# Chunked scan and two gated layers on one core: decays spread in float32, fillers on TensorE, 512-column tiles and a new early order

## The chip, the cores and the metric

The kernel runs on one core of a Trainium2 chip. The metric is the device time of one execution in microseconds (us), measured outside the kernel; the profile gives the span from the first to the last instruction of one profiled execution, which is a little shorter.

## What is computed

Three stages, cut to what matters:

```python
# 1. chunked scan, for each batch (4) and head (8); S = 768, D = 32, N = 16
log_a = np.log(np.clip(a, 1e-06, 1.0))
# per chunk: cum = cumsum(log_a), L = exp(cum_i - cum_j) for i >= j
y = ((C @ B.T) * L) @ x + (C @ state) * exp(cum)
state = exp(cum_last) * state + sum_j B_j x_j exp(cum_last - cum_j)
# 2. gated layer, 3072 tokens, 256 -> 1536 -> 256
g = x @ w_gate; x = (g * sigmoid(g) * (x @ w_val)) @ w_out
# 3. squared-ReLU layer, 256 -> 2048 -> 256
h = np.maximum(x @ w_in, 0.0); out = (h * h) @ w_out2
```

The weights arrive as 64-bit floats and are turned into float32 on the chip.

## The kernel before

**Scan.** `chunks` cuts each batch of 768 tokens into six chunks of 112 and one of 96, 28 in all, worked in order by `chunk_ops`. For chunk k TensorE forms the scores `cb` (B times C), VectorE's scan (L578 for a half of four heads, L608 for all eight) forms the decays `L`, VectorE multiplies both into `mt` (L662, two halves), and TensorE's product `ys` (L676) of `mt` and `xa` gives the chunk's output and its next state, which goes through `st`, `turn` (L715) and back into `xa` (L718). There is one `mt` buffer. The first seven chunks (`EARLY`, batch 0) get the input of their scan in a special way: the clipped decays are cut into three bfloat16 parts that add up to the float32 value (`part_steps`, L251 to L261, on ScalarE and VectorE), and TensorE spreads them over 128 partitions with a 0/1 matrix `pick` (L569, eight matmuls a chunk); chunk 0 instead loads its decays with a broadcast DMA (L594) and clips them (L604). Later chunks load a broadcast copy from `decay` in DRAM.

**Gated layer.** `glu` works on one slice f of 128 hidden features (12 slices) and n tokens: products `g` and `v` (L729), tanh on ScalarE (L793), two VectorE operations (L796, L799), and the product `acc` (L847). In the "exact" form it uses plain float32 matmuls, 2 + 2 + 2 instructions of n columns (two passes each in the trace); otherwise both operands are cut into a high and a low part and it takes 6 + 6 + 6 matmuls of n columns, and GpSimd forms the low part of `t` (L820). Batch 0 is cut into cells (`PLAN["cells"]`: two slices, a range of chunks, exact or not). Batches 1 to 3 are done in tiles of 336 and 432 tokens.

**Weights.** A `Unit` is 1 MB of weights: two DMAs, two ScalarE operations (L406, L400), three on VectorE (L412, L417, L421); a split into high (L427, ScalarE) and low (L432, GpSimd) follows. Nine units feed the gated layer.

**Squared-ReLU layer.** `relu2`: per slice and 512 tokens six matmuls of 512 columns (`h`, L729) and twelve of 256 (`acc`, L920). At the end four `drain` operations copy the last accumulators into buffers of pool `tmp` (three buffers) and `store` sends them out (L955).

**Order.** `Graph.order` is a list planner: with a cost for each operation, priorities from `PLAN` and a count of buffers, it fixes in advance the order in which each engine's instructions stand. The engines then run their queues strictly in that order, with semaphores.

Of the kernel before, what the change touches and what calls it, by code (L numbers as in the profile page):

```python
# [34 lines left out]
class Graph:  # L35
# [14 lines left out]
    def order(self):  # L50
# [5 lines left out]
        avail, out, events, now = {}, [], [], 0.0  # L56
# [71 lines left out]
def kernel(  # L128
# [45 lines left out]
    pools = dict(w=20, raw=2, tmp=3, p=3, tr=3, L=2, ab=2, xf=1, bcr=1, st=2, ps=8)  # L174
# [7 lines left out]
    NBC, NX, NEB = 4, 3, 2  # L182
# [3 lines left out]
    pools["mt"] = 1  # L186
# [14 lines left out]
    decay = dram.tile([NB, NCB, H, Q + 1], F32, name="decay")  # L201

    def new(buf, shape, dtype, tag=None):
# [24 lines left out]

    def clip():
# [4 lines left out]
        nc.vector.tensor_scalar(  # L234
            dv[:, :full, 1:], ac[0 : 3 * R, : full * Q].rearrange("p (c q) -> p c q", c=full),
            1e-6, 1.0, op0=ALU.max, op1=ALU.min,
        )
        if full < NCB:
            nc.vector.tensor_scalar(
                dv[:, full, 1 : 1 + S - full * Q], ac[0 : 3 * R, full * Q : S],  # L240
                1e-6, 1.0, op0=ALU.max, op1=ALU.min,
            )

    e3 = ac[0 : 3 * R, : EARLY * (Q + 1)].rearrange("p (c q) -> p c q", c=EARLY)

    def part_steps(c0, c1):

        d, e, q = dv[:, c0:c1], e3[:, c0:c1], parts3[:, c0:c1]

        def one():  # L250
            nc.scalar.activation(q, d, AF.Copy)  # L251

        def two():
            nc.vector.tensor_tensor(e, d, q, op=ALU.subtract)

        def three():
            nc.scalar.activation(q[R : 2 * R], e[R : 2 * R], AF.Copy)
            nc.scalar.activation(q[2 * R :], e[2 * R :], AF.Copy)

        def four():  # L260
            nc.vector.tensor_tensor(q[2 * R :], e[2 * R :], q[2 * R :], op=ALU.subtract)  # L261

        return one, two, three, four

    def setup_pool():
        nc.gpsimd.memset(eye, 0.0)
# [24 lines left out]
    def setup_delta():  # L291
        nc.gpsimd.memset(delta, 0.0)
# [6 lines left out]
    def setup_pick():  # L299
        nc.gpsimd.memset(pick, 0.0)  # L300
        for i in range(3):
            nc.gpsimd.affine_select(
                out=pick, in_=pick, pattern=[[-1, H]], base=-i * R,
                channel_multiplier=1, compare_op=ALU.not_equal, fill=1.0,
            )
# [11 lines left out]
    def setup_mt():  # L317
        nc.gpsimd.memset(mt[:, :, Q:P], 0.0)

    xf_buf = Buf("xf")  # L320
    op_eye = g.add("POOL", 550, setup_pool, prio=-1000)
    op_eb = [g.add("POOL", 350, lambda i=i: setup_eb(i), prio=-999.5 + 0.1 * i) for i in range(NEB)]
    op_mask = g.add("POOL", 600, setup_mask, prio=-999)
    op_delta = g.add("POOL", 2000, setup_delta, prio=-998)
    op_mt = g.add("POOL", 200, setup_mt, prio=-997)
    op_pick = g.add("POOL", 900, setup_pick, prio=-996)
    op_bc = g.add("POOL", 1500, setup_bc, prio=-900)
    op_tab = g.add("ACT", 1500, act_table, prio=-990)
    op_pick.deps.append(op_tab)

    def dma(eng, n, cost, move, fn, deps=(), prio=0.0, bufs=()):

        i = g.add(eng, n * cost, fn, deps, prio, bufs, lat=0)
        return g.add("DMA", move, None, [i], prio, bufs, lat=1700)

    ld_a = dma("SP", 3, 450, 400, load_a, [], -950, setup_L)
    op_clip = g.add("DVE", 1250, clip, [ld_a], -950, setup_L)

# [5 lines left out]
    parts_done = {}  # L344
    first_parts = 3
    for c0, c1, prio in ((0, first_parts, -940), (first_parts, EARLY, 150)):
        f = part_steps(c0, c1)
        n = (c1 - c0) * (Q + 1)
        o1 = g.add("ACT", 220 + n * 0.83, f[0], [op_clip], prio, setup_L)
        o2 = g.add("DVE", 160 + n * 1.04, f[1], [o1], prio, setup_L)  # L350
        o3 = g.add("ACT", 2 * (220 + n * 0.83), f[2], [o2], prio, setup_L)
        o4 = g.add("DVE", 160 + n * 1.04, f[3], [o3], prio, setup_L)
        for c in range(c0, c1):
            parts_done[c] = o4
    kept = {
        b: dma("SP", 1, 450, 400, lambda b=b: keep_decays(b), [op_clip], 300 + b, setup_L)
# [84 lines left out]
    def chunk_ops(k, prio, after=(), load_after=()):  # L441
# [9 lines left out]
        c.mt = Buf("mt")  # L451
# [6 lines left out]
        load_after = [*load_after, before.load if before else None]  # L458
        free_x = ck[k - NX].y if k >= NX else None
        free_m = before.y if before else None  # L460
# [100 lines left out]
        if early and k:  # L561
            for i in range(HG):
                ps = Buf("ps")

                def spread(i=i, ps=ps):
                    v = new(ps, [P, G, Q + 1], F32, "ab")
                    for j in range(G):
                        h = i * G + j
                        nc.tensor.matmul(  # L569
                            v[:, j, :], pick[:, h : h + 1].to_broadcast([3 * R, P]), parts3[:, k, :],  # L570
# [12 lines left out]
                o = g.add("PE", 250, spread, [parts_done[k], op_pick, ck[k - 1].scans[-1]], prio, [ps, c.L], lat=250)  # L583
                s = g.add("DVE", 1080, scan, [o, op_delta, *scans], prio, [ps, c.L])
                scans = [s]
        else:
            ab = Buf("ab")

            def load_ab():
                v = new(ab, [P, H, Q + 1], F32, "ab")  # L590
                if early:
                    nc.vector.memset(v[:, :, 0:1], 0.0)
                    w = a[b, :, t : t + n]
                    nc.sync.dma_start(out=v[:, :, 1:], in_=bass.AP(w.tensor, w.offset, [[0, P], *w.ap]))  # L594
                else:
                    w = decay[b, t // Q].rearrange("h q -> (h q)")
                    nc.sync.dma_start(
                        out=v.rearrange("p h q -> p (h q)"),
                        in_=bass.AP(w.tensor, w.offset, [[0, P], *w.ap]),
                    )  # L600

            def hold():
                v = ab.t[:, :, 1:]
                nc.vector.tensor_scalar(v, v, 1e-6, 1.0, op0=ALU.max, op1=ALU.min)  # L604
# [494 lines left out]
```

## Time and profile before

| | us |
|---|---|
| device time, median of 3 runs | 674.58 (674.35 to 675.39) |
| the profiled execution, device time | 675.3 |
| its span | 673.6 |
| TensorE (PE) busy | 641.3, 95% |
| VectorE (DVE) busy | 418.6, 62% |
| ScalarE (ACT) busy | 337.7, 50% |
| GpSimd (POOL) busy | 224.1, 33% |

A busy share is an average over the span. The page's 40 slices show PE at 10, 60, 80 and 90% in its first four slices (17 us each), and at 90% or more from there to the last slice (60%). PEld is the loading of stationary operands and overlaps PE. Ends of matmuls are modelled, so that short gaps between matmuls count as busy; start times are recorded.

### The profile page before, as it was taken

What the parts mean: (1) busy time and instruction counts of PE and PEld (TensorE: products, weight loads), DVE (VectorE), ACT (ScalarE), POOL (GpSimd) and SP (SyncE); (2) the same over time, 40 slices, a digit from 0 to 9 for tenths busy, and PEclk for the clock granted to TensorE, in tenths of its full rate; (3) what the DMA queues carried; (4) which work ended last, traced back from release to release, by engine and by line L of the source; (5) the groups of instructions that cost most, each with busy time, mean ns of one, the idle gap of its engine ahead of it and who ended that gap; (6) DMA issues with size and microseconds to landing.
All of it is one profiled execution on the core that took longest, in us unless ns stands there. A gap on an engine that the chain in (4) does not pass through costs nothing.

```text
span 673.6 us, 11146 instructions
## 1 busy us (share of the span) xinstructions
PE 641.3 (95%) x4318; PEld 575.9 (85%) x4318; DVE 418.6 (62%) x598; ACT 337.7 (50%) x666; POOL 224.1 (33%) x226
## 2 busy tenths in 40 slices
PE   1689899999999999999999999999999999999996
PEld 1476498998998899988999989999999999999996
DVE  6899875456666665666468788554454544544543
ACT  6775554344545544545366665444444444444443
POOL 4353447546556564666255751100000000000000
PEclk9979999999999999999999999999999999999999
DMA  8868675206574747342521430000000000000000
GB/s 236 186 154 171 130 163 85 46 5 133 107 141 79 143 76 143 72 91 46 157 63 63 133 119 1 0 32 1 1 32 1 31 1 1 32 1 1 32 1 32
DMA packets 135749, 49.55 MB, mean 74 GB/s; under 512 B 121136, under 2 KB 124208, under 8 KB 135696
## 3 DMA queue, kind: packets, MB, share of 16 engines
q1 hardware_dynamic: 135408, 48.57, 32.6%
q8 instruction: 34, 0.56, 0.4%
q10 hardware_dynamic: 288, 0.26, 0.1%
q14 instruction: 19, 0.16, 0.1%
HBM read 34.59 MB, written 3.22 MB: 56 GB/s over the span
## 4 chain that ended last, share of the span: by engine, by line
PE 88%; DMA 4%; POOL 3%; ACT 2%; DVE 1%; SPq 1%; issue 1%; DVEq 0%; ACTq 0%; POOLq 0%
PE acc L920 20%; PE h L729 20%; PE g L729 15%; PE acc L847 14%; PE v L729 13%; PE ys L676 2%; POOL p L820 2%; DMA raw<-in_moe_w_val_dram 2%; PE cb L647 1%; DMA eb<-in_B_dram 1%; POOL lo L432 1%; PE cb L638 1%; DMA bct<-bcs 1%; PE turn L715 1%; ACT raw L406 1%
## 5 line engine op out<-in xcount | busy, mean ns | idle before, releaser
L920 PE MATMUL acc<-hi,p 128*128 128x256 f32 x768 | 152.5, 283 | 0.0
L820 POOL TENSOR_TENSOR p<-t,p 128x432 fp32r<-128x432 f32 (+2 forms) x88 | 102.5, 1168 | 103.7 <-ACT p L815 95.1
L920 PEld LDWEIGHTS acc<-hi,p 128*128 128x128 f32 x768 | 125.5, 191 | 4.0
L901 DVE TENSOR_TENSOR t<-t 128x512 f32<-128x512 f32 x96 | 69.8, 728 | 70.5 <-ACT t L898 70.4
L920 PE MATMUL acc<-lo,p 128*128 128x256 f32 x384 | 108.6, 283 | 0.0
L908 DVE TENSOR_TENSOR p<-t,p 128x512 fp32r<-128x512 f32 x96 | 66.2, 691 | 55.1 <-ACT p L904 54.9
L898 ACT ACTIVATE t<-h 128x512 f32<-128x512 f32 x96 | 57.2, 597 | 81.9 <-PE h L729 80.4
L796 DVE SCALAR_TENSOR_TENSOR t<-t,g 128x432 f32<-128x432 f32 (+3 forms) x102 | 53.4, 524 | 64.3 <-ACT t L793 63.6
L847 PE MATMUL acc<-p,hi 128*128 128x432 f32 (+2 forms) x352 | 92.2, 342 | 1.0 <-POOL p L820 0.9
L904 ACT ACTIVATE p<-t 128x512 fp32r<-128x512 f32 x96 | 60.5, 631 | 62.9 <-DVE t L901 61.7
L793 ACT ACTIVATE t<-g 128x432 f32<-128x432 f32 (+3 forms) x102 | 47.7, 469 | 58.2 <-PE g L729 56.3
L920 PEld LDWEIGHTS acc<-lo,p 128*128 128x128 f32 x384 | 73.4, 191 | 3.9
L729 PE MATMUL h<-xh_all,hi 128*128 128x512 f32 x192 | 76.5, 398 | 0.0
L729 PE MATMUL h<-xh_all,lo 128*128 128x512 f32 x192 | 76.2, 397 | 0.0
L729 PE MATMUL h<-xl_all,hi 128*128 128x512 f32 x192 | 76.2, 397 | 0.0
L815 ACT ACTIVATE p<-t 128x432 fp32r<-128x432 f32 (+2 forms) x88 | 45.6, 519 | 60.9 <-DVE t L799 59.2
L847 PEld LDWEIGHTS acc<-p,hi 128*128 128x128 f32 x352 | 61.9, 188 | 6.1 <-POOL p L820 2.4
L799 DVE SCALAR_TENSOR_TENSOR t<-t,v 128x432 f32<-128x432 f32 (+1 forms) x90 | 50.1, 557 | 26.0 <-PE v L729 19.6
L729 PE MATMUL g<-xh_all,hi 128*128 128x432 f32 (+2 forms) x184 | 64.3, 349 | 0.0
L729 PE MATMUL g<-xh_all,lo 128*128 128x432 f32 (+2 forms) x184 | 62.1, 337 | 0.4 <-POOL lo L432 0.4
L729 PE MATMUL g<-xl_all,hi 128*128 128x432 f32 (+2 forms) x184 | 61.8, 336 | 0.0
L432 POOL TENSOR_TENSOR lo<-v,hi 128x1024 fp32r<-128x1024 f32 x17 | 45.0, 2650 | 45.7 <-ACT hi L427 43.0
(97 smaller groups left out, 1165.1 us busy)
## 6 DMA issues: line engine op xcount, KB each, us to landing
ab<-decay SPq DMA_DIRECT2D x21, 452.0 KB, 4.7
raw<-in_moe_w_out_dram SPq DMA_DIRECT2D x14, 512.0 KB, 5.1
raw<-in_moe_w_in_dram SPq DMA_DIRECT2D x8, 512.0 KB, 4.4
raw<-in_moe_w_gate_dram SPq DMA_DIRECT2D x6, 512.0 KB, 4.1
raw<-in_moe_w_val_dram SPq DMA_DIRECT2D x6, 512.0 KB, 6.2
xa<-in_x_dram SPq DMA_DIRECT2D x24, 112.0 KB, 2.5
out_dram<-o SPq DMA_DIRECT2D x10, 256.0 KB, 2.2
bc<-in_B_dram SPq DMA_DIRECT2D x18, 56.0 KB, 4.3
```

The source lines that it names most:

```text
L432: e.tensor_tensor(self.lo.t, self.v.t, self.hi.t.bitcast(F32), op=ALU.subtract)
L729: nc.tensor.matmul(ps, l, r, start=(i == 0), stop=(i == len(terms) - 1))
L793: nc.scalar.activation(t[:, :n], gg(), AF.Tanh, scale=0.5)
L796: nc.vector.scalar_tensor_tensor(tb.t[:, :n], tb.t[:, :n], 1.0, gg(), op0=ALU.add, op1=ALU.mult)
L799: nc.vector.scalar_tensor_tensor(tb.t[:, :n], tb.t[:, :n], 0.5, vv(), op0=ALU.mult, op1=ALU.mult)
L820: e.tensor_tensor(p[:, 1, :n], tb.t[:, :n], p[:, 0, :n].bitcast(F32), op=ALU.subtract)
L847: nc.tensor.matmul(ps, l, r, start=bank not in done_f, stop=f == NF - 1, skip_group_check=True,)
L898: nc.scalar.activation(new(tb, [P, TN], F32, "t"), ph.t, AF.Relu)
L901: nc.vector.tensor_tensor(tb.t, tb.t, tb.t, op=ALU.mult)
L904: nc.scalar.activation(new(pb, [P, 2, TN], F32R, "p")[:, 0, :], tb.t, AF.Copy)
L908: e.tensor_tensor(pb.t[:, 1, :], tb.t, pb.t[:, 0, :].bitcast(F32), op=ALU.subtract)
L920: nc.tensor.matmul(ps, pb.t[:, l, tk], r, start=(f == 0 and s == 0 and q % 2 == 0), stop=(f == NF2 - 1 and s == 2), skip_group_check=True,)
```

## The change

- The decays are held once, in float32 and on all 128 partitions (`dv_all`; the rows above 32 are zeros), loaded straight into place by two DMAs and clipped there. The cutting into three parts, chunk 0's broadcast load and its clip are gone. All seven early chunks spread their decays on TensorE with a float32 `pick` matrix, 56 matmuls instead of 48 in bfloat16.
- Two `mt` buffers instead of one; four `tmp` buffers instead of three.
- Batches 1 to 3 in tiles of 256 and four times 512 tokens instead of six tiles of 336 and 432.
- Fillers: where the planner sees TensorE idle for 110 ns or more in its first 70 us, it puts matmuls of a bfloat16 tile of zeros (`idle`, 256 columns, one per 110 ns) ahead of the operation that waits, into the buffer that this operation then overwrites: 119 of them.
- Some clearing of tiles moves from GpSimd to VectorE ahead of the first data; planner costs and the starting clock change; one PSUM bank is no longer kept free; and `PLAN` is new, so that the early order of all engines differs.

The diff, cut to its core:

```diff
-    pools = dict(w=20, raw=2, tmp=3, p=3, tr=3, L=2, ab=2, xf=1, bcr=1, st=2, ps=8)
+    pools = dict(w=20, raw=2, tmp=4, p=3, tr=3, L=2, ab=2, xf=1, bcr=1, st=2, ps=8)
-    mt = const.tile([P, H, P], F32, name="mt")
+    mts = [const.tile([P, H, P], F32, name=f"mt{i}") for i in range(NMT)]
+    idle = const.tile([P, 256], BF16, name="idle")
-    pick = const.tile([3 * R, H], BF16, name="pick")
-    parts3 = const.tile([3 * R, EARLY, Q + 1], BF16, name="parts3")
+    pick = const.tile([P, H], F32, name="pick")
+    dv_all = const.tile([P, NCB, Q + 1], F32, name="dv")
+    dv = dv_all[0:R]
...
+        if buf.pool == "ps" and fills:
+            t = buf.t.rearrange("p a b -> p (a b)") if len(shape) == 3 else buf.t
+            t = t[:, : min(n, 256)]
+            for _ in range(fills.pop()):
+                nc.tensor.matmul(t, idle[:, : shape[0]], idle[:, : t.shape[-1]], start=True, stop=True)
...
-        free_m = before.y if before else None
+        free_m = ck[k - NMT].y if k >= NMT else None
...
-        if early and k:
+        if early:
...
-                            v[:, j, :], pick[:, h : h + 1].to_broadcast([3 * R, P]), parts3[:, k, :],
+                            v[:, j, :], pick[:, h : h + 1].to_broadcast([P, P]), dv_all[:, k, :],
...
-    tiles = [(b * S + o, b * S + e) for b in range(NB) for o, e in ((0, cut), (cut, S))]
+    over = (T - S) % TN
+    edges = [0, cut, S, *([S + over] if over else []), *range(S + over + TN, T + 1, TN)]
+    tiles = list(zip(edges, edges[1:]))
...
+            if op.eng == "PE":
+                if op.start < PLAN["warm"]:
+                    free = max([last] + [o.start + o.took + 250 for o in op.after if o is not None])
+                    if op.start - free >= 110:
+                        fills.append(int((op.start - free) / 110))
+                last = op.start + op.took
...
     cells=[
+        (5, 3, 7, 0),
+        (4, 0, 3, 0),
+        (5, 0, 3, 1),
...
+    spare=0,
+    warm=70000,
```

What it does to the queues, at the three places that matter below. First VectorE from the clip of the decays to the second chunk's `mt`. The rows before (L412, L417, L421 are one weight unit's three operations, L578 and L608 scans, `parts` the cutting into three):

```order
L254 TENSOR_TENSOR ac<-dc,parts_110 96x452
L261 TENSOR_TENSOR parts_110<-ac,parts_110 32x339
L412 SCALAR_TENSOR_TENSOR raw<-raw 128x1024
L417 TENSOR_SCALAR v<-v 128x1024
L421 SCALAR_TENSOR_TENSOR v<-v,raw 128x1024
L261 TENSOR_TENSOR parts_110<-ac,parts_110 32x452
...
L604 TENSOR_SCALAR ab<-ab 128x8x112
L608 SCALAR_TENSOR_TENSOR L<-ab,delta 128x904
L662 TENSOR_TENSOR mt<-cb,L 128x4x112 x2
L578 SCALAR_TENSOR_TENSOR L<-ab,delta 128x452 x2
```

And now, where L561 is the scan of a half, L634 the multiplication into `mt` and L395, L400, L404 the unit's three:

```order
L561 SCALAR_TENSOR_TENSOR L<-ab,delta 128x452 x2
L395 SCALAR_TENSOR_TENSOR raw<-raw 128x1024
L400 TENSOR_SCALAR v<-v 128x1024
L404 SCALAR_TENSOR_TENSOR v<-v,raw 128x1024
L561 SCALAR_TENSOR_TENSOR L<-ab,delta 128x452 x2
L634 TENSOR_TENSOR mt_107<-cb,L 128x4x112 x2
...
L671 TENSOR_TENSOR xl_all<-ys,xh_all 128x2x112
L561 SCALAR_TENSOR_TENSOR L<-ab,delta 128x452
L634 TENSOR_TENSOR mt_108<-cb,L 128x4x112 x2
```

The first scan has moved ahead of all weight work, the second ahead of the first `mt`, and two units instead of two units and six cutting and clipping operations stand ahead of the second `mt`.

Second, TensorE just behind the second chunk's product (`ys` with `mt_108`), now (L701 are the products `g`, L819 `acc`, L552 the spreading of decays, L610 the scores):

```order
L648 MATMUL ys<-mt_108,xa_105 32x128 x8
L701 MATMUL g<-xf,v 128x112 x6
L687 MATMUL turn<-eye,st 16x128 x2
L701 MATMUL g<-xf,v 128x112 x2
L819 MATMUL acc<-t,v 128x112 x2
L701 MATMUL g<-xf,v 128x112 x4
...
L701 MATMUL g<-xf,v 128x224 x4
L468 MATMUL trb<-eye,eb_101 128x128 x2
L610 MATMUL cb<-bct 128x112 x8
L819 MATMUL acc<-t,v 128x224 x4
```

Exact products of the first two chunks fill this stretch, which before held far fewer of them. Between the second and the seventh chunk's product there now stand 42 exact instructions of 112 columns and 12 of 224, 32 spreading matmuls, 18 split ones of 336 and 24 fillers; before there stood 22 exact of 112 and 2 of 336, 32 spreading and 36 split ones of 224.

Third, GpSimd's low parts of weights (`lo`). Before, each stands between other work:

```order
L432 TENSOR_TENSOR lo<-v,hi 128x1024
L622 TENSOR_TENSOR mt<-eb_100,L 128x8x16
L432 TENSOR_TENSOR lo<-v,hi 128x1024
L622 TENSOR_TENSOR mt<-eb_101,L 128x8x16
L820 TENSOR_TENSOR p<-t,p 128x224
```

Now six of the nine stand in one run, ahead of the two steps (L518, L521) that the first late chunk's transposition needs, and of the first low parts of `t` (L792):

```order
L594 TENSOR_TENSOR mt_108<-eb_101,L 128x8x16
L509 TENSOR_TENSOR bcr<-bc_99,bcs 128x256
L415 TENSOR_TENSOR lo<-v,hi 128x1024 x6
L518 TENSOR_TENSOR bcs<-bcr,bcs 128x8x32
L521 TENSOR_TENSOR bcs<-bcr,bcs 128x8x2x16
L792 TENSOR_TENSOR p<-t,p 128x336 x2
```

## Rows read from the trace of the kernel before

**Rows 1.** Stretches: length, busy PE, PEld, DVE, ACT, POOL, granted clock, DMA share, GB/s.
```profile
0.00:25.76 25.76, 8.67 (x74) 6.72 (x75) 17.46 (x25) 14.98 (x29) 12.09 (x34) 1.00 0.91 224
25.76:59.33 33.57, 27.71 (x298) 23.03 (x297) 31.90 (x50) 26.22 (x69) 13.90 (x13) 0.90 0.73 157
59.33:673.60 614.27, 604.94 (x3949) 546.10 (x3948) 369.28 (x526) 296.46 (x569) 198.11 (x180) 1.00 0.29 63
```

**Rows 2.** Timeline of PE: products of the second and seventh chunk (start, length, instruction).
```profile
25.76 0.64 PE L676 MATMUL ys<-mt,xa 128*32 128x128 f32 x16
...
59.33 0.64 PE L676 MATMUL ys<-mt,xa 112*32 112x128 f32 x16
```

**Rows 3.** Granted clock in one stretch, and the same scores twice on PE's timeline.
```profile
36.00:38.00 2.00, 1.64 (x8) 1.37 (x8) 2.00 (x3) 0.46 (x1) 1.55 (x1) 0.50 1.14 274
...
22.56 2.06 PE L638 MATMUL cb<-bct 64*128 64x112 f32 x16
...
43.38 1.15 PE L638 MATMUL cb<-bct 64*128 64x112 f32 x16
```

**Rows 4.** Timeline of PE: starts from which the prices per matmul come.
```profile
54.04 0.60 PE L729 MATMUL g<-xf,v 128*128 128x112 f32 x4
54.47 0.56 PE L569 MATMUL ab<-parts,pick 96*128 96x113 bf16 x8
54.97 0.64 PE L676 MATMUL ys<-mt,xa 128*32 128x128 f32 x16
...
301.18 0.36 PE L729 MATMUL g<-xl_all,hi 128*128 128x432 f32 x1
...
302.94 0.35 PE L729 MATMUL v<-xl_all,hi 128*128 128x432 f32 x1
...
450.98 0.28 PE L920 MATMUL acc<-hi,p 128*128 128x256 f32 x1
...
452.42 0.40 PE L729 MATMUL h<-xh_all,hi 128*128 128x512 f32 x1
...
453.82 0.28 PE L920 MATMUL acc<-hi,p 128*128 128x256 f32 x1
```

**Rows 5.** Timeline of ACT and DVE: the first unit's arrival, a scan, `mt`, `xl_all`.
```profile
7.98 1.13 ACT L406 ACTIVATE raw<-raw 128x1024 int32<-128x1024 uint16 x1 [0.71 <-DMA raw<-in_moe_w_val_dram]
...
16.65 2.04 DVE L608 TENSOR_TENSOR_SCAN L<-ab,delta 128x904 f32<-128x904 f32 x1
18.79 1.15 DVE L662 TENSOR_TENSOR mt<-cb,L 128x448 f32<-128x448 f32 x2
...
23.43 0.39 DVE L699 TENSOR_TENSOR xl_all<-ys,xh_all 128x224 fp32r<-128x224 f32 x1
```

**Rows 6.** Timeline of DVE: the three operations of one weight unit, GpSimd idle beside them.
```profile
29.50 1.22 DVE L412 SCALAR_TENSOR_TENSOR raw<-raw 128x1024 uint32<-128x1024 uint32 x1
30.63 0.69 DVE L417 TENSOR_SCALAR v<-v 128x1024 f32<-128x1024 f32 x1
31.35 1.23 DVE L421 SCALAR_TENSOR_TENSOR v<-v,raw 128x1024 uint32<-128x1024 uint32 x1
```

**Rows 7.** Timeline of POOL, DVE, PE: the same operations beside GpSimd's, and PE's waits.
```profile
65.67 4.19 POOL L432 TENSOR_TENSOR lo<-v,hi 128x1024 fp32r<-128x1024 f32 x1 [4.81 <-ACT hi L427]
...
71.17 2.35 POOL L432 TENSOR_TENSOR lo<-v,hi 128x1024 fp32r<-128x1024 f32 x1
...
68.33 2.60 DVE L412 SCALAR_TENSOR_TENSOR raw<-raw 128x1024 uint32<-128x1024 uint32 x1
...
71.37 2.69 DVE L417 TENSOR_SCALAR v<-v 128x1024 f32<-128x1024 f32 x1
...
71.50 1.72 PE L847 MATMUL acc<-t,v 128*128 128x432 f32 x4 [1.11 <-DVE t L799]
...
77.73 1.72 PE L847 MATMUL acc<-t,v 128*128 128x432 f32 x4 [1.61 <-DVE t L799]
```

**Rows 8.** Timeline of the end: the last of the four copies out.
```profile
670.38 0.42 DVE L951 COPY o<-acc 128x256 f32<-128x256 f32 x1 [1.69 <-DMA out_dram<-o]
```

More of the change, by code (lines that the diff above doesn't have):

```diff
@@ L55, in order @@
         free = {p: [None] * n for p, n in self.pools.items()}
-        avail, out, events, now = {}, [], [], 0.0
+        avail, out, events, now = {}, [], [], 850.0
         busy = {}
@@ L185 @@
     pools.update({f"eb{i}": 1 for i in range(NEB)})
-    pools["mt"] = 1
+    pools.update({f"mt{i}": 1 for i in range(NMT)})
     g = Graph(pools)
@@ L233, in clip, with load_a, setup_dve @@
             nc.vector.memset(dv[:, full, 1 + S - full * Q :], 0.0)
-        nc.vector.tensor_scalar(
-            dv[:, :full, 1:], ac[0 : 3 * R, : full * Q].rearrange("p (c q) -> p c q", c=full),
-            1e-6, 1.0, op0=ALU.max, op1=ALU.min,
+        r = R
+        while r < P:
+            nc.vector.memset(dv_all[r : 2 * r], 0.0)
+            r *= 2
+    def load_a():
+        v = a.rearrange("b h s -> (b h) s")
+        nc.sync.dma_start(
+            out=dv[:, :full, 1:], in_=v[:, : full * Q].rearrange("p (c q) -> p c q", c=full)
         )
         if full < NCB:
[L239 to L263, printed above, removed]
+            nc.sync.dma_start(out=dv[:, full, 1 : 1 + S - full * Q], in_=v[:, full * Q :])
+    def clip():
+        for v in (dv[:, :full, 1:], dv[:, full:, 1 : 1 + S - full * Q]):
+            nc.vector.tensor_scalar(v, v, 1e-6, 1.0, op0=ALU.max, op1=ALU.min)
+    def setup_dve():
+        nc.vector.memset(eye, 0.0)
+        nc.vector.memset(delta, 0.0)
+        for m in mts:
+            nc.vector.memset(m[:, :, Q:P], 0.0)
     def setup_pool():
-        nc.gpsimd.memset(eye, 0.0)
         nc.gpsimd.affine_select(
@@ L300, in setup_pick @@
         nc.gpsimd.memset(pick, 0.0)
[L301 to L305, printed above, removed]
+        nc.gpsimd.affine_select(
+            out=pick, in_=pick, pattern=[[-1, H]], base=0,
+            channel_multiplier=1, compare_op=ALU.not_equal, fill=1.0,
+        )
     def setup_bc():
@@ L342, in keep_decays @@
         )
[L344 to L354, printed above, removed]
     kept = {
-        b: dma("SP", 1, 450, 400, lambda b=b: keep_decays(b), [op_clip], 300 + b, setup_L)
+        b: dma("SP", 1, 450, 400, lambda b=b: keep_decays(b), [op_clip], 300 + b)
         for b in range(1, NB)
@@ L450, in chunk_ops @@
         c.L = Buf("L")
-        c.mt = Buf("mt")
+        c.mt, mt = Buf(f"mt{k % NMT}"), mts[k % NMT]
         if prev is not None:
@@ L590, in load_ab @@
                 v = new(ab, [P, H, Q + 1], F32, "ab")
[L591 to L604, printed above, removed]
+                w = decay[b, t // Q].rearrange("h q -> (h q)")
+                nc.sync.dma_start(
+                    out=v.rearrange("p h q -> p (h q)"),
+                    in_=bass.AP(w.tensor, w.offset, [[0, P], *w.ap]),
+                )
             def scan():
@@ L611, in scan @@
                 )
-            o = dma("SP", 1, 480, 2300 if early else 1650, load_ab, [*load_after, kept.get(b)], ldp, [ab])
-            if early:
-                o = g.add("DVE", 640, hold, [o], prio, [ab])
+            o = dma("SP", 1, 480, 1650, load_ab, [*load_after, kept[b]], ldp, [ab])
             scans = [g.add("DVE", 2060, scan, [o, op_delta, *after, before.scans[-1] if before else None], prio, [ab, c.L])]
@@ L1009 @@
         if f == 0:
-            deps += [ck[k].x for k in range(EARLY, NK) if tl[0] <= chunks[k][0] * S + chunks[k][1] < tl[1]]
+            at0 = [bb * S + tt for bb, tt, _ in chunks]
+            deps += [ck[k].x for k in range(EARLY, NK) if at0[k] < tl[1] and at0[k] + chunks[k][2] > tl[0]]
         step_ops.append(glu(tl, f, 0, tl[1] - tl[0], False, 20000 + s * 10, deps)[0])
```

85 lines of the change are left out of this document (40 added, 45 removed).

## The prediction

> **What bounds the kernel now.** I read the 40 slices first: TensorE is full from the sixth slice on, so the time is TensorE's work plus what it loses early. Then I cut the span at two marks on TensorE's timeline [rows 2], the products of the second chunk (25.76 us) and of the seventh (59.33), and read busy times by stretch [rows 1]. Ahead of the first mark TensorE is busy 8.67 of 25.76 us: it waits for the chain decays, scan, `mt`. Between the marks it is busy 27.71 of 33.57 and VectorE 31.90: VectorE is the bound there, at 95%. Behind the second mark TensorE is busy 604.94 of 614.27. So TensorE is idle for 23.0 us in the first 59, and for 9.3 in the rest.
>
> The clock costs something too. In one stretch the granted clock is 0.50, that is 1.2 of 2.4 GHz, and eight score instructions take 2.06 us at 22.56 but 1.15 at 43.38 [rows 3]. Between the marks the mean grant is 0.90 [rows 1]: a fifth of the stretch at half speed. With TensorE busy most of that time, it lost some 2.7 us, so its work between the marks is 27.71 - 2.7 = 25.0 us at full clock.
>
> **Prices.** From starts on TensorE's timeline [rows 4]: four records (two instructions) of exact 112 columns take 0.43 us, 0.215 an instruction; eight bfloat16 spreading matmuls 0.50, 0.0625 each. Nine split matmuls of 432 columns take 1.76, 0.196 each or 0.453 ns a column; six of 512 take 1.40, 0.456 ns a column; twelve of 256 take 1.44, 0.120 each or 0.469 ns a column. A price per column that hardly depends on the width decides the tiles of 512.
>
> **Part by part.**
> *Spreading in float32.* No row shows it. The nearest is the exact matmul of 112 columns, which is float32 too: 0.215 us. Below, it cannot cost less than the bfloat16 one, 0.0625. I take 0.215, since type and width agree. 56 x 0.215 - 48 x 0.0625 = 9.0 us more on TensorE.
> *Cells.* Exact columns go from 1760 to 2096 per pair of slices, 672 more column-slices in all. Exact costs six instructions, 11.5 ns a column; split 18 matmuls, 8.2. At most 2.2 us more.
> *Tiles.* A slice is 18 matmuls of n columns. Before: 3 x 12 x 18 x (336 + 432) columns; now 12 x 18 x (256 + 4 x 512), the same 497,664 columns; only the 256 wide ones cost a little more, some 0.6 us. There are 60 slices instead of 72, so fewer changes from one group to the next; of the 9.3 us idle behind the second mark I give back 1.0.
> TensorE's work so grows by 9.0 + 2.2 + 0.6, at most 11.8 us; I take 11.2, with the exact surplus nearer the middle. The change pays only if TensorE loses over 11 us less.
>
> *Up to the first mark.* The first scan ran at 16.65, behind two weight units and six operations for the decays [rows 5]. Now it stands first. The fillers delay it: 32 of them from about 1.2 us, at 0.120 each (256 columns) if the clock is up and 0.24 if not, end between 5 and 9; with the first half of the spreading behind them I start VectorE at 8.0, about the middle. Then its queue up to the second chunk's `mt`: scan 2.04, unit 1.22 + 0.69 + 1.23 = 3.14 [rows 6], scan 2.04, `mt` 1.15, unit 3.14, copy-out 0.39 and half a scan 1.02, `mt` 1.15 [rows 5], together 14.1. That gives 22.1 for the mark, 3.7 earlier. ScalarE waited for the first unit's weights until 7.98 [rows 5], and that load is now first among the weights, so it doesn't come last. Bounds: 20.5 if the fillers run at full clock, 25.76 if a later load holds it. The 24 spreading matmuls, 5.2 us, lie in time that TensorE spent waiting.
>
> *Between the marks.* TensorE's list changes by: exact 42 x 0.215 + 12 x 0.43 = 14.2 against 22 x 0.215 + 2 x 0.645 = 6.0, so +8.2; spreading 32 x (0.215 - 0.0625) = +4.9; split 18 of 336 (2.8) against 36 of 224 (3.8), so -1.0. That is +12.0, and 24 fillers at 0.120, +2.9. With 25.0 this makes 39.9 us. VectorE's list for the stretch loses one half scan, one L412 and one L417 and gains two short gates: 31.90 - 1.0 - 1.2 - 0.7 + 0.5 = 29.5. The bound moves from VectorE to TensorE, whose list is 10 us longer, so I add no waits; short gaps are in the busy time already. The second `mt` buffer is part of this: scores of the next chunk need not wait for the product before. The seventh chunk's product is then at 22.1 + 39.9 = 62.0. Bounds: 37 if the fillers only stand in gaps, 45.8 if the 5.9 us of idle stay.
>
> *Behind the second mark.* Of the 11.2 us, 4.6 were spent ahead of the first mark (24 spreading instead of 16, one exact pair) and 12.0 between; so 5.4 less is left here. Four `tmp` buffers also cure the end: the last copy waits 1.69 us for a store to leave one of three buffers [rows 8]; with a fourth it doesn't, -1.7. The five fillers here cost 0.6. 614.3 - 5.4 - 1.7 - 1.0 + 0.6 = 606.8.
>
> *GpSimd's row of six `lo`.* Beside such an operation VectorE's L412 took 2.60 instead of 1.22 and L417 2.69 instead of 0.69, and TensorE waited 1.11 and 1.61 us for the gates behind them [rows 7]. In the sum I leave this at what it cost before. The Trainium skill, GPSIMD Engine Reference, section 1 (Specifications), says that GpSimd's SBUF interfaces are shared with VectorE and that they contend with VectorE instructions that have two SBUF inputs or run in a two-port mode. The trace agrees, with 2.60 against 1.22 [rows 6, 7]. By that rule each weight operation of VectorE that meets the row of six is stretched, and the sum would come out as in the first rival.
>
> Other edits cost nothing that I can see: the clearing on VectorE runs before any data is there, the two loads of the decays replace three, and one broadcast load is gone.
>
> **Sum.** 62.0 + 606.8 = 668.8 us of span, against 673.6. The profiled execution took 675.3, 1.7 more than its span, and the median of the runs is 0.7 below it: 668.8 + 1.7 - 0.7 = **669.8 us**.
>
> **Rivals.**
> *Slower: six `lo` in a row hold VectorE.* Place: the stretch just behind the second mark, where weight units 7 to 9 and the gates of exact cells share VectorE. Price: 1.4 + 2.0 = 3.4 us for two weight operations [rows 6, 7]; three such pairs, for six `lo`, are 10.2, of which 3.4 are in the sum. All of the rest passes to TensorE if VectorE has no lead: 669.8 + 6.8 = 676.6. It decides if the run of six starts before the exact cells are through, that is if VectorE's L395 and L400 there average over 2 us. For it: TensorE's two waits [rows 7]. Against: VectorE's list is 10 us shorter than TensorE's just ahead. Chance 0.15.
> *No gain: the waits between the marks stay.* If TensorE still idles 5.9 us there, because queues in a fixed order wait for each other and not for the longer list, the time is 675.7. Chance 0.10.
> *Slower by the clock.* If the fillers don't raise it, the 90 fillers and 24 spreading matmuls ahead of the first mark, 10.8 + 5.2 = 16.0 us at full clock, take twice as long and the mark comes 16 us later: 686. Against: the clock had come back by 43.38 [rows 3]. Chance 0.03.
> *Better.* First mark at 20.5 and fewer losses between: 664 to 666. Chance 0.12, inside faster.
> *It doesn't do what it says.* The wide tiles buy no price per column [rows 4]; that is in the sum at 1.0 us and nothing more hangs on it.
>
> **How the numbers follow.** The forecast has 0.60, from 666 to 673 by the bounds above. A measurement of this kernel tells 0.2% (1.35 us) from no change. Faster: 0.60 + 0.12 and a part of the second rival, 0.75; within 0.2%: 0.10; slower: 0.15, the first and third rival less their mild ends. The range leaves out the clock rival and the best and worst tails: 663.5 to 677.0.
>
> **What would show it.** Right: the first scan near 8, the second product near 22.1, the seventh near 62, TensorE busy over 90% between them; spreading matmuls start 0.43 us apart in pairs; the last copy without a wait; late tiles at 0.456 ns a column. Wrong: the second product later than 25, VectorE still at 95% between the marks, waits of TensorE for gates of over 5 us behind the second mark, or scores at 2 us behind 15.

## The result, and the profile after

The changed kernel takes 664.07 us (median of 4 runs, 663.71 to 665.70) against 674.99 for the kernel before beside it: a ratio of 0.984 (95% interval 0.983 to 0.985), 10.9 us faster. The forecast was 669.8 us, in a range that holds the result. The direction was right; the gain was forecast at 5.2 us, less than half of its size. The profiled execution took 664.27 us, its span is 662.48.

The three stretches of the forecast, cut at the products of the second and the seventh chunk; columns as in [rows 1], the same stretches of the kernel before:

```profile
0.00:24.45 24.45, 22.21 (x201) 19.16 (x201) 17.52 (x28) 10.40 (x22) 7.55 (x28) 1.00 0.82 183
24.45:64.46 40.01, 38.56 (x394) 34.86 (x394) 35.26 (x57) 28.92 (x73) 9.13 (x9) 1.00 0.68 158
64.46:662.48 598.02, 593.98 (x3704) 506.88 (x3703) 362.70 (x495) 289.96 (x541) 205.27 (x171) 1.00 0.29 64
```

The first mark is 2.4 us late (forecast 22.1), the middle is right (39.9 forecast, TensorE busy 96% of it; VectorE, though, is busy for 35.26 us where 29.5 were forecast), and the stretch behind the second mark is 8.8 us shorter than forecast (606.8). To see where, I cut that one at the first matmul of the last layer. First the kernel before, then the changed one:

```profile
59.33:393.46 334.13, 329.93 (x2209) 296.76 (x2209) 220.82 (x318) 169.23 (x362) 188.94 (x176) 1.00 0.48 102
393.46:673.60 280.14, 275.01 (x1741) 249.34 (x1739) 148.46 (x209) 127.23 (x208) 9.18 (x5) 1.00 0.05 16
```

```profile
64.46:385.06 320.60, 320.55 (x1965) 258.64 (x1965) 213.95 (x287) 162.10 (x334) 196.35 (x167) 1.00 0.50 105
385.06:662.48 277.42, 273.43 (x1741) 248.24 (x1739) 148.75 (x209) 127.85 (x208) 8.92 (x4) 1.00 0.05 16
```

Three things stand out. In the first of the two stretches, TensorE's idle time (length less busy) has gone from 4.20 us to 0.05. In the second, where TensorE is idle only behind the last matmul, it has gone from 5.13 to 3.99. And the last layer, with the same 1741 records, keeps TensorE busy for 273.43 instead of 275.01 us, although the change doesn't touch it. Something has changed the price of a column.

The timeline of the start shows fillers, spreading, and what holds the second chunk's product:

```profile
1.14 5.90 PE L225 MATMUL ab<-idle 128*128 128x256 bf16 x32 [1.14 <-DVE idle L207]
6.87 1.94 PE L552 MATMUL ab<-dv,pick 128*128 128x113 f32 x16
8.65 1.58 PE L225 MATMUL ab<-idle 128*128 128x256 bf16 x13
...
12.06 2.24 PE L225 MATMUL cb<-idle 128*128 128x256 bf16 x19
...
17.93 0.64 PE L648 MATMUL ys<-mt,xa 128*32 128x128 f32 x16
...
8.03 2.09 DVE L561 TENSOR_TENSOR_SCAN L<-ab,delta 128x452 f32<-128x452 f32 x2 [3.07 <-PE ab L552]
20.78 1.14 DVE L634 TENSOR_TENSOR mt<-cb,L 128x448 f32<-128x448 f32 x2
...
22.98 1.10 ACT L389 ACTIVATE raw<-raw 128x1024 int32<-128x1024 uint16 x1 [3.65 <-DMA raw<-in_moe_w_val_dram]
23.99 0.36 ACT L690 ACTIVATE xa<-turn 16x256 f32<-16x256 f32 x1
...
24.45 0.65 PE L648 MATMUL ys<-mt,xa 128*32 128x128 f32 x16 [1.10 <-issue]
```

VectorE is through with the second `mt` at 21.92, as forecast. But ScalarE's queue stands for 3.65 us at a weight that has not landed, and the copy of the state `xa`, which the product also needs, is queued behind it.

GpSimd's row of `lo` (five of the six; the sixth runs at 76.73) and its neighbours, the place of the slower rival:

```profile
60.24 14.13 POOL L415 TENSOR_TENSOR lo<-v,hi 128x1024 fp32r<-128x1024 f32 x5 [6.40 <-ACT hi L410]
...
60.40 3.31 DVE L404 SCALAR_TENSOR_TENSOR v<-v,raw 128x1024 uint32<-128x1024 uint32 x1
...
65.14 1.37 DVE L400 TENSOR_SCALAR v<-v 128x1024 f32<-128x1024 f32 x1
...
67.72 2.10 DVE L395 SCALAR_TENSOR_TENSOR raw<-raw 128x1024 uint32<-128x1024 uint32 x1
...
72.51 2.94 DVE L404 SCALAR_TENSOR_TENSOR v<-v,raw 128x1024 uint32<-128x1024 uint32 x1
...
71.45 1.61 PE L701 MATMUL g<-xf,v 128*128 128x432 f32 x4
72.90 1.61 PE L701 MATMUL v<-xf,v 128*128 128x432 f32 x4
74.35 1.61 PE L819 MATMUL acc<-t,v 128*128 128x432 f32 x4
```

The collision is there: 3.31, 2.10 and 2.94 us where such operations took 1.22 and 1.23, and 1.37 where one took 0.69 [rows 6]. But TensorE's `acc` at 74.35 has no wait, where the `acc` of [rows 7] had 1.11 and 1.61. In the kernel before, an `acc` stands right behind the products of its own slice:

```profile
73.06 1.61 PE L729 MATMUL v<-xf,v 128*128 128x432 f32 x4
74.51 1.61 PE L729 MATMUL g<-xf,v 128*128 128x432 f32 x4
77.73 1.72 PE L847 MATMUL acc<-t,v 128*128 128x432 f32 x4 [1.61 <-DVE t L799]
```

Now the products of a second slice stand between a slice's products and its `acc`, so the gates (ScalarE's and VectorE's work that turns `g` and `v` into the input of `acc`) have 2.9 us more.

### The profile page after: what moved, and what is told of

It reads as the page before. It is cut to its first block, busy times and chain, and to the rows that moved or that the text cites. A ratio compares the mean times of both kernels' runs of the same rounds, so it can differ in the third digit from the quotient of the medians.

```text
span 662.5 us, 10931 instructions
## 1 busy us (share of the span) xinstructions
PE 654.8 (99%) x4297; PEld 560.9 (85%) x4297; DVE 415.5 (63%) x578; ACT 329.3 (50%) x634; POOL 221.9 (34%) x207
## 4 chain that ended last, share of the span: by engine, by line
PE 97%; DMA 1%; SPq 0%; ACT 0%; issue 0%; DVE 0%; ACTq 0%
PE acc L892 21%; PE h L701 20%; PE g L701 18%; PE acc L819 16%; PE v L701 13%; PE ys L648 2%; PE ab L552 1%; PE cb L619 1%; DMA raw<-in_moe_w_val_dram 1%; PE ab L225 1%; PE cb L610 1%; PE turn L687 1%; PE g L225 1%; PE cb L225 0%; PE trb L225 0%
## 5 line engine op out<-in xcount | busy, mean ns | idle before, releaser
L792 POOL TENSOR_TENSOR p<-t,p 128x512 fp32r<-128x512 f32 (+4 forms) x74 | 98.0, 1326 | 91.4 <-ACT p L787 89.3
L768 DVE SCALAR_TENSOR_TENSOR t<-t,g 128x512 f32<-128x512 f32 (+6 forms) x92 | 51.9, 565 | 71.1 <-ACT t L765 71.0
L819 PE MATMUL acc<-p,hi 128*128 128x512 f32 (+4 forms) x296 | 85.7, 372 | 0.0
L701 PE MATMUL h<-xh_all,hi 128*128 128x512 f32 x192 | 75.8, 395 | 0.0
L701 PE MATMUL h<-xl_all,hi 128*128 128x512 f32 x192 | 75.8, 395 | 0.0
L701 PE MATMUL h<-xh_all,lo 128*128 128x512 f32 x192 | 74.7, 389 | 0.0
L787 ACT ACTIVATE p<-t 128x512 fp32r<-128x512 f32 (+4 forms) x74 | 42.2, 571 | 62.5 <-DVE t L771 58.9
L765 ACT ACTIVATE t<-g 128x512 f32<-128x512 f32 (+6 forms) x92 | 46.1, 503 | 45.3 <-PE g L701 42.6
L701 PE MATMUL g<-xh_all,hi 128*128 128x512 f32 (+4 forms) x176 | 64.4, 366 | 0.0
L701 PE MATMUL g<-xh_all,lo 128*128 128x512 f32 (+4 forms) x176 | 61.4, 349 | 0.0
L701 PE MATMUL g<-xl_all,hi 128*128 128x512 f32 (+4 forms) x176 | 61.3, 349 | 0.0
L819 PEld LDWEIGHTS acc<-p,hi 128*128 128x128 f32 x296 | 52.1, 188 | 10.3 <-issue 2.9
L771 DVE SCALAR_TENSOR_TENSOR t<-t,v 128x512 f32<-128x512 f32 (+2 forms) x66 | 42.9, 649 | 21.6 <-PE v L701 17.2
```

What stands on the lines that cost most here:

```text
L701: nc.tensor.matmul(ps, l, r, start=(i == 0), stop=(i == len(terms) - 1))
L765: nc.scalar.activation(t[:, :n], gg(), AF.Tanh, scale=0.5)
L768: nc.vector.scalar_tensor_tensor(tb.t[:, :n], tb.t[:, :n], 1.0, gg(), op0=ALU.add, op1=ALU.mult)
L771: nc.vector.scalar_tensor_tensor(tb.t[:, :n], tb.t[:, :n], 0.5, vv(), op0=ALU.mult, op1=ALU.mult)
L792: e.tensor_tensor(p[:, 1, :n], tb.t[:, :n], p[:, 0, :n].bitcast(F32), op=ALU.subtract)
L819: nc.tensor.matmul(ps, l, r, start=bank not in done_f, stop=f == NF - 1, skip_group_check=True,)
```

## Experiments

Theory at the start: the surplus behind the second mark comes from the wide tiles (fewer ns a column), the early gain from the order and the clock. Rival: the tiles buy nothing, as forecast, and the fillers' clock does it.

### The price of a column

**Old tiles in the changed kernel.**

```diff
-    edges = [0, cut, S, *([S + over] if over else []), *range(S + over + TN, T + 1, TN)]
-    tiles = list(zip(edges, edges[1:]))
+    tiles = [(b * S + o, b * S + e) for b in range(NB) for o, e in ((0, cut), (cut, S))]
```

> The changed kernel with its tiles of 512 tokens put back to 336 and 432; the order of TensorE up to about 95 us stays as it is. Theory (width): in the changed kernel 512 columns take 227 ns, 0.443 ns a column, where 336 and 432 took 0.458 and 0.455; that is 3.4 us over the gated layer and 1.5 more in the last layer's h. Then this kernel takes 3.4 to 4.9 us more than the changed one's 664.1: 667.5 to 669. Rival (the forecast's own price): the width buys nothing per column and only fewer slices, so 664.1 to 665. In its trace the h matmuls of the last layer tell whether their price (231 ns after, 233.5 before) hangs on the tiles: 233.5 here if so.

Measured 670.63, ratio to before 0.993 (0.992 to 0.995): the tiles are worth some 6.5 us in the changed kernel, more than the theory. Its two stretches behind the second mark:

```profile
63.98:391.73 327.75, 325.13 (x2181) 292.24 (x2181) 214.11 (x313) 165.78 (x360) 194.18 (x179) 1.00 0.47 103
391.73:668.83 277.10, 273.12 (x1741) 248.25 (x1739) 149.05 (x209) 128.22 (x208) 9.12 (x5) 1.00 0.05 16
```

The first is 7.15 us longer than with the wide tiles, of which 2.6 are waits of TensorE. But the last layer stays at 273.12 us busy: what it gained doesn't come from the tiles.

**New tiles in the kernel before**, alone; then with the last layer's weights asked for as early as in the changed kernel; then with its pace of the chunks too.

```diff
-    pace=[-3, 2.85, 8],
-    second=[53, 4, 0],
+    pace=[-5, 2.65, 13],
+    second=[34, 5, 6],
```

> The kernel before with the tiles of 256 and four times 512 tokens alone; TensorE's order up to about 95 us stays as it is. Theory (width): 3.4 to 4.9 us less than before's 675.0, so 670 to 671.6. Rival (the forecast's price): 0.4 less, 674.6. If the wide tiles only pay together with the second batch of edits (four tmp buffers, no kept bank), it is not faster at all.

> The kernel before with the new tiles, and with the last layer's weights asked for as early as in the changed kernel (second = 34, 5, 6 instead of 53, 4, 0). Theory: what made the new tiles alone 13 us slower was that the weights of the last layer, timed in steps of the tiles, came late: TensorE waited for lo and for the squares between 400 and 425 us and lost clock there. With them early the tiles are worth what they are in the changed kernel, 6.5: 667.5 to 670. Rival: those waits come from the three tmp buffers or the kept bank and stay: over 680.

> The kernel before with the new tiles and the changed kernel's numbers for both things that are timed in steps of the tiles: the chunks (pace) and the last layer's weights (second). Theory: with the weights alone it stood at 679.5 because TensorE waited 2.20 us at 173.7 for GpSimd's p and then ran at half clock from 175 to 181; GpSimd was late by the chunk work, so the new pace cures it and the tiles show their worth: 668 to 672. Rival: the wait comes from elsewhere and stays: 678 to 680.

Measured 688.36 (ratio 1.019, 1.017 to 1.020), 679.49 (1.007, 1.006 to 1.008) and 675.42 (1.001, 1.001 to 1.002). The first is 13 us slower: loads that are timed in steps of the tiles come late when there are fewer steps. TensorE's waits at the start of the last layer, then the stretch behind them:

```profile
405.76 0.50 PE L729 MATMUL h<-xh_all,lo 128*128 128x512 f32 x1 [1.66 <-POOL lo L432]
410.98 0.38 PE L920 MATMUL acc<-hi,p 128*128 128x256 f32 x1 [2.66 <-ACT p L904]
```

```profile
412.00:418.00 6.00, 5.88 (x25) 5.37 (x26) 5.97 (x6) 2.69 (x3) 2.80 (x1) 0.50 0.00 1
```

After them the granted clock is 0.50 for six us, the lower level. The two timing edits take away 8.9 and 4.1 us, in the direction of the theory, but neither run came into its range (667.5 to 670, and 668 to 672), and what is left is no gain at all, where 6.5 was expected. With both edits, the stretch from the second mark to the last layer reads:

```profile
59.29:393.34 334.05, 328.12 (x1993) 263.33 (x1993) 218.84 (x292) 164.87 (x335) 189.92 (x164) 1.00 0.49 102
```

The wide tiles took 1.81 us off TensorE's busy time there (329.93 before), and its waits grew by 1.73 (4.20 to 5.93). In these kernels a 512-column matmul of the gated layer takes 231 ns at the median, in the changed one 227.

**64 bytes.** A part of what is left is where things lie. The changed kernel's constants are larger by 6,208 bytes a partition (its tiles, each rounded up to 32 bytes), which is 48 and a half times 128. The buffers behind them (weights, `p`, `tmp`) so begin at 73,856 bytes, 577 times 128; before they began at 67,648, 64 bytes past a multiple of 128. These addresses are worked out from the program; no trace shows them. One unused tile of 64 bytes among the constants swaps that, and in the traces every engine's order stays as it was:

```diff
+    pad = const.tile([P, 16], F32, name="pad")
```

> The changed kernel with an unused tile of 64 bytes a partition among the constants: weights and the parts p then begin 64 bytes past a multiple of 128, as before; nothing else differs. Theory (address): the last layer's h matmuls go from 231 back to 233.5 ns (576 of them, 1.5 us) and the gated layer's 512-column ones from 227 to 231 (864 of them, 3.5 us): 664.1 + 5 = 669. Rival: the addresses don't matter, 664.1, and the price came with the order of the work.

> The kernel before with the same 64 bytes: weights and p begin at a multiple of 128. Theory (address): h goes from 233.5 to 231, 1.5 us, and the tiles of 336 and 432 hardly change (their medians were the same in both programs): 675.0 - 1.5 = 673.5. Rival: no difference, 675.0.

> The kernel before with the new tiles, the new pace and weights early (675.4 without the padding), and the 64 bytes. Theory (address): the 512-column matmuls of the gated layer go from 231 to 227 (3.5 us) and h from 233.5 to 231 (1.5): 670.4. Rival: no difference, 675.4.

Measured: the changed kernel with the padding 668.23 (ratio to before 0.990, 0.988 to 0.991), 4.2 us slower; the kernel before with it 673.51 (0.998, 0.997 to 0.999), 1.3 faster; the kernel before with new tiles 672.25 (0.996, 0.994 to 0.997), 3.2 faster than without. Of the three theories (669, 673.5 and 670.4), the second came true; the other two had the right sign and 0.8 and 1.9 us too much. The stretches of the padded changed kernel, from the second mark to the last layer and from there on:

```profile
65.86:389.10 323.24, 322.98 (x1965) 257.88 (x1965) 211.14 (x285) 162.24 (x333) 194.07 (x167) 1.00 0.49 105
389.10:668.04 278.94, 274.95 (x1741) 247.42 (x1739) 148.76 (x209) 127.79 (x208) 8.84 (x4) 1.00 0.05 15
```

The last layer is back at 274.95 us. (The second mark is also 1.4 us later, 65.86 against 64.46; in this execution the clock fell at 58 us, to a mean of 0.96 between the marks.) In the kernel before with the padding it went the other way, to 273.14; below its two stretches stands the first one of the kernel before with padding and new tiles:

```profile
58.49:392.53 334.04, 330.39 (x2209) 296.92 (x2209) 220.83 (x318) 169.31 (x362) 189.03 (x176) 1.00 0.47 102
392.53:670.77 278.24, 273.14 (x1741) 248.30 (x1739) 148.48 (x209) 127.14 (x207) 9.20 (x5) 1.00 0.05 16
...
59.64:391.92 332.28, 326.72 (x1994) 263.54 (x1993) 219.02 (x292) 164.55 (x335) 189.54 (x164) 1.00 0.49 102
```

These rows also say why the wide tiles are worth 6.5 us in one kernel and only 1.3 in the other (672.25 against 673.51), both with the buffers at a multiple of 128. TensorE's busy time in this stretch falls by about as much: 3.67 us here (330.39 to 326.72) and 4.58 in the changed kernel (325.13 to 320.55). But its waits grow by 1.91 here (3.65 to 5.56) and shrink by 2.57 there (2.62 to 0.05).

Starts on TensorE's timeline give the price; the changed kernel without the padding (18 matmuls from the first to the second row), then with it (21):

```profile
353.77 0.39 PE L701 MATMUL g<-xh_all,hi 128*128 128x512 f32 x1
...
357.86 0.39 PE L819 MATMUL acc<-p,hi 128*128 128x512 f32 x1
```

```profile
343.81 0.39 PE L702 MATMUL v<-xh_all,hi 128*128 128x512 f32 x1
...
348.71 0.62 PE L820 MATMUL acc<-p,hi 128*128 128x512 f32 x2
```

4.09 / 18 = 0.227 us against 4.90 / 21 = 0.233. With the order unchanged, and the effect reversed in the kernel before, the address is the cause; which of the buffers it is was not tried.

### Fillers and the clock

**No fillers; 18 ahead of the first spreading alone; half of them.** `warm=0`; a cap of 18 and `warm=5000`; or one filler per 220 ns.

```diff
-    warm=70000,
+    warm=0,
```

> The changed kernel without its 119 fillers; the order of all else is the same. Theory (clock): the fillers stand in time that TensorE waits for data, and their worth is the clock: without them the granted clock falls to 0.5 for a part of the first 60 us as it did before (where it cost some 2.7 us between the marks), and the time is 666 to 670. Rival 1: the 29 fillers behind the first mark are paid by TensorE, which is the bound there, and the clock stays up by the real work: 660.5 to 663. Rival 2: both hardly matter, 664.

> The changed kernel with 18 fillers ahead of the very first spreading matmul and no others. In the changed kernel fillers run at 213 ns from 1.14 to 5.6 us and at 109 from then on, and the decays are there at 4.99; without fillers the first 29 spreading records run at 213 ns, up to 11.3 us. Theory: 18 fillers end just when the decays are there, the clock is up at about 5.7, VectorE's first scan starts near 6.1 instead of 7.1, and nothing else is delayed: 661 to 662.4, at or under the 662.4 without fillers. Rival: the second product waits for a load of x or of weights whatever the scan does: 662.4.

> The changed kernel again, to stand beside the next two on one chip: 664.1.

> The changed kernel without fillers, again. Theory: the planned fillers ahead of the first scores and of the second transposition take longer than the wait that they fill and push the first chunk's product from 15.66 to 17.93, so the kernel without them is 1 to 2 us faster than the changed one of the same batch. Rival: no difference over 0.7 us.

> The changed kernel with one filler per 220 ns of planned wait instead of one per 110, 55 or so instead of 119. Theory (their number is the cost): between the two others, about 663. Rival (the clock): if fillers are worth having for the clock, half of them keep it up and cost nothing, and this is the fastest of the three, under 662.

Without fillers: 662.39 (ratio 0.982, 0.980 to 0.983), and 662.63 when run beside the changed kernel, which took 663.50 there. The second pair differs by 0.9 us; its single runs don't overlap (662.0 to 663.4 and 663.4 to 664.4), its ratios do. With 18 it is 662.62, with half of them 663.84, level with all 119, where the theory that their number is the cost had put it at about 663. The first theory's 666 to 670 without fillers did not come; its first rival's 660.5 to 663 did. So the fillers gain nothing; the two versions below the changed kernel are faster by about 1 us, which is at the edge of what a measurement can tell. The fillers do hold the clock up: its mean over the span was 0.999 or 1.000 in seven of nine executions of the changed kernel, and in three of nine without fillers, where the others had 0.992 to 0.997. The time without them was lower all the same. The start without them:

```profile
4.99 6.79 PE L552 MATMUL ab<-dv,pick 128*128 128x113 f32 x32 [4.99 <-DVE dv L255]
11.61 0.38 PE L468 MATMUL trb<-eye,eb 128*128 128x128 f32 x2
12.61 1.21 PE L610 MATMUL cb<-bct 64*128 64x112 f32 x16 [0.61 <-ACT bct L477]
...
15.66 0.91 PE L648 MATMUL ys<-mt,xa 128*32 128x128 f32 x16 [0.59 <-POOL mt L594]
...
21.92 0.64 PE L648 MATMUL ys<-mt,xa 128*32 128x128 f32 x16 [1.57 <-DMA xa<-in_x_dram]
```

The spreading itself runs slowly here, 32 records in 6.62 us (4.99 to 11.61) instead of 16 in 1.78 (6.87 to 8.65 above), and yet the first chunk's product is at 15.66 instead of 17.93: planned fillers last longer than the waits that they fill. (Ahead of the scores, 19 of them take 2.2 us, where the wait without them is 0.61.)

**A wait on purpose.** In the kernel without fillers TensorE waits once, in the middle of the wide tiles, for copies by VectorE (2 or 7):

```diff
+            if s == 0 and tl == tiles[4] and f == 6:
+                q = pg.t[:, :256]
+                nc.tensor.matmul(q, idle[:, :P], idle, start=True, stop=True)
+                for _ in range(7):
+                    nc.vector.tensor_copy(idle, q)
+                nc.tensor.matmul(q, idle[:, :P], idle, start=True, stop=True)
```

> The changed kernel without fillers, in which TensorE waits once in the middle of the wide tiles (in the third tile behind batch 0) for two copies of VectorE from PSUM, about 1.2 us. Theory: a short wait costs itself and the clock stays up: 1.2 to 1.5 more than 662.4, 663.6 to 664. Rival: any wait lowers the clock behind it: over 665.

> The same with seven copies, a wait of about 3.2 us. Theory: a long wait is paid twice, once as idle time and once as a stretch at half clock behind it, as behind the waits of 2.20 and 2.62 us in two of the earlier runs (each followed by 4 to 6 us at 0.5, a loss of 2 to 3 us): 5.5 to 6.5 more than 662.4, 668 to 669. Rival: it costs its own length, 665.6.

The short one, 0.98 us in the trace, gave 664.16: 1.8 more, and no fall of the clock behind it. The long one gave 667.79, 5.4 more, just under the theory's 668 to 669; but its six runs fall into two groups, 665.4 to 666.0 and 669.6 to 670.2. The lower group lies at the rival's 665.6, the wait's own length. In its execution of 665.43 us the mean granted clock was 1.000, so the clock did not fall behind the wait there. The profiled execution is of the upper group:

```profile
254.28:257.55 3.27, 0.00 (x0) 0.00 (x1) 2.97 (x7) 0.30 (x1) 1.22 (x1) 0.80 1.16 217
257.55:264.00 6.45, 6.45 (x18) 5.11 (x19) 1.38 (x2) 0.71 (x2) 0.00 (x0) 0.57 0.05 10
```

```profile
260.30 0.63 PE L701 MATMUL v<-xh_all,hi 128*128 128x512 f32 x1
260.73 0.63 PE L701 MATMUL v<-xl_all,hi 128*128 128x512 f32 x1
```

A wait of 3.27 us, then matmuls of 512 columns 0.43 us apart: fourteen of them (257.60 to 263.44) at 0.19 us too much, 2.7 us, so nearly the wait's length again. (This execution has a second fall of the clock, at 58 to 62 us, so the gap between the groups is not the price of one fall.) A wait of this length can take the clock down, and does not each time.

### Order, kept bank, spreading, end

**The old early plan** (`chunk_at`, `unit_at`, `split_at`, `cells` of before, no fillers).

> The changed kernel without fillers, and with chunk_at, unit_at, split_at and cells of before: all code of the change, but the old early order. Theory (order): what TensorE gained in the first 100 us comes from the order, so its waits come back in part: some 3 to 6 us more than the 662.4 without fillers, 665 to 668.5. Rival (code): the float32 spreading, the second mt buffer and the single load of the decays gain it in any order: 662 to 664.

Measured 673.49 (0.999, 0.998 to 1.000): 11.1 us more than with the new plan, twice what was expected. Against the kernel before, all the code of the change in the old order leaves about 1 us, which is hardly to be told from none. The wide tiles and the address are in that sum, and the old numbers were never fitted to the new code; so the run shows that the change needs a new plan, and not how many of its 10.9 us are the order's. One of its waits, and the clock behind it:

```profile
18.53 1.14 PE L648 MATMUL ys<-mt,xa 128*32 128x128 f32 x16 [3.09 <-POOL mt L594]
```

```profile
18.00:24.00 6.00, 5.47 (x43) 4.50 (x44) 5.52 (x9) 3.90 (x10) 2.73 (x2) 0.50 1.03 225
```

**One bank kept free** (`spare=1`, no fillers).

> The changed kernel without fillers and with one PSUM bank kept free again, as before. Theory (lead): with the eighth bank TensorE's products g and v stand further ahead of their acc, and that is why the gates of the exact cells no longer hold it (before it waited 1.11 and 1.61 us for them): with the bank kept free such waits return, 2 to 4 us more than 662.4, 664.5 to 666.5. Rival: the lead comes from the order of cells alone: 662.4.

Measured 693.88 (1.029, 1.028 to 1.031), far outside both. The planner lays out another order, in which TensorE waits 11.07 us for GpSimd at 72:

```profile
63.83 11.71 POOL L415 TENSOR_TENSOR lo<-v,hi 128x1024 fp32r<-128x1024 f32 x4
...
83.10 1.14 PE L648 MATMUL ys<-mt,xa 128*32 128x128 f32 x16 [11.07 <-POOL mt L594]
```

It doesn't isolate the lead of the products over their `acc`, which so stays argued from the rows. It does show that the numbers of the plan did not carry over to another set of buffers.

**Spreading of four chunks twice** (no fillers).

```diff
+                        for _ in range(2 if k >= 3 else 1):
```

> The changed kernel without fillers, in which the spreading matmuls of the fourth to the seventh chunk are issued twice, 32 more instructions of 0.222 us. Theory: TensorE is the bound between the marks, so all of it is paid: 7.1 more than 662.4, 669.5. Rival: a part lies in waits (2.3 us of idle time there without fillers): 667 to 668.5. If VectorE is still the bound there, under 2.

Measured 666.08 (0.988, 0.986 to 0.989), 3.7 to 4.1 more, below the theory's 7.1 and below the rival's range. Between the marks, without the doubling and with it:

```profile
21.92:60.57 38.65, 36.31 (x371) 32.67 (x371) 33.78 (x54) 27.20 (x72) 7.60 (x9) 1.00 0.70 163
21.30:64.33 43.03, 42.82 (x434) 39.75 (x434) 34.83 (x55) 28.12 (x72) 7.88 (x9) 1.00 0.64 151
```

It is 43.03 us instead of 38.65: of 7.1 us added, 4.4 are paid there. Most of the rest goes into TensorE's waits, 2.3 us (38.65 less 36.31 busy) before and 0.2 now. TensorE is the bound there, but with some slack.

**Four `tmp` buffers in the kernel before.**

```diff
-    pools = dict(w=20, raw=2, tmp=3, p=3, tr=3, L=2, ab=2, xf=1, bcr=1, st=2, ps=8)
+    pools = dict(w=20, raw=2, tmp=4, p=3, tr=3, L=2, ab=2, xf=1, bcr=1, st=2, ps=8)
```

> The kernel before with four tmp buffers instead of three; the order differs only from about 370 us on. Theory: the last copy no longer waits 1.69 us for a store, and the stretch from the last matmul to the end goes from 5.1 to 4.0 us as in the changed kernel: 1.1 to 1.7 less than 675.0, 673.3 to 673.9. Rival: the last store's own latency sets the end whatever the copies do, 675.0.

Measured 674.89 against 675.21 (0.999, 0.998 to 1.000): the rival's number, no change. In the trace the end is 4.07 us instead of 5.13 and the last copy doesn't wait for a store; the time shows no more than a hint of it.

## Why the forecast was right and where it failed

- *First scan near 8, spreading at 0.215 us:* right; 8.03 (which had been taken as the middle of a range), and sixteen records (eight instructions) in 1.78 us, 0.222 each.
- *Second product at 22.1:* measured 24.45 (23.59 in the trace of the second run of the changed kernel). VectorE's sum was right to 0.2 us; that the first unit's weights come early said nothing of the third's, for which ScalarE stood with `xa` behind it. That case was the upper bound of the term.
- *Between the marks 39.9:* 40.01. TensorE as the bound is borne out by the doubled spreading, with some slack. That the number fits so well is partly luck: TensorE's list took 38.56 us and its waits, forecast as none, 1.45. And VectorE's list, forecast at 29.5, took 35.26, so it was not 10 us shorter than TensorE's; one weight operation beside GpSimd's row took 3.31 instead of 1.23.
- *The slower rival:* its collisions came, its price did not. VectorE's L400 and L395 just behind the second mark took 1.37 and 2.10 us, under the average of 2 that the rival asked for, and TensorE had other products to do meanwhile; that this second point decided it is argued from the rows.
- *Behind the second mark 606.8:* this is the step that failed, by 8.8 us, in three terms.
  - "A price per column that hardly depends on the width" took the prices of before for those of after (some 4.0 us of the 8.8). With 64 bytes of shift they fell: the padded kernel is 4.2 us slower, and its stretches are 2.6 longer in the gated layer (323.24 against 320.60) and 1.5 in the last layer.
  - "Of the 9.3 us idle I give back 1.0", and 1.7 for the end (2.6 of the 8.8): 5.3 came back, since TensorE's waits went almost altogether (4.15) and the end gave 1.1. With the old tiles in the changed kernel 2.62 us of those waits remain, so the wide tiles have a share in it.
  - The gated layer's busy time (2.2 of the 8.8) fell by 6.95 at the old addresses (329.93 to 322.98), where work moved ahead, less fillers, was to give 4.8. The tiles, put at 0.6 us more work, took 1.8 less in the kernel before, which is about the size of this term.
- *Fillers raise the clock:* they do, ahead of 6.87; without them the spreading does it, and the scores at 12.61 take 1.21 us, not 2.06 as in [rows 3]. What they gain there they lose by standing in front of work that is ready. Behind the start the clock fell again in six of nine executions without fillers and in two of nine with them, and the times without them were lower even so.

## What to carry to other kernels

A stretch that a change doesn't touch is the control: where its matmuls take another time, look for what moved, here 64 bytes in front of every working buffer. A wait of TensorE of two or three us can cost its length again in clock. Fillers that kept the clock up were worth nothing here, since they stood in front of work that was ready; that products kept well ahead of their `acc` are the better cure is what the rows suggest, and no run isolates it. What is timed in steps of a tile has to be timed anew when the tile grows.

## What the hardware did that I had not expected

- Buffers 64 bytes past a multiple of 128 made the gated layer's 512-column matmuls take 231 to 233 ns at the median instead of 227, and the last layer 275.0 to 275.4 us instead of 273.1 to 273.4, in both kernels and in both directions. Widths of 336 and 432 columns did not change visibly (153 and 196 ns at the median in the kernel before, with the padding and without).
- The view prints a granted clock of 1.00 in the first stretch while matmuls run at half speed. It is a gap in the record: the traces hold no granted clock before 5.75 us in the changed kernel, 11.27 without fillers and 24.60 in the kernel before. The starts show the level: without fillers the first spreading records start 0.21 us apart, later ones 0.11, and the scores in [rows 3] took 2.06 and 1.15.
- Behind waits of TensorE of 2.66, 3.09 and 3.27 us the granted clock fell to 0.50 for six or seven us; behind the single one of 0.98 it did not. The length alone doesn't decide: in one execution with the wait of 3.27 us put in (665.43 us) the mean clock was 1.000, and in the execution of the short wait the clock fell to 0.50 from 16 to 22 us, behind waits of 0.61 and 0.97.
